# Batch 0 of an attention-and-FFN kernel: K and Q loaded by token halves, four-head chains, and new planner durations

## The chip, the cores and the metric

The kernel runs on one core of a Trainium2 chip. Its engines are TensorE (PE, matmuls; its weight loads are listed as PEld), VectorE (DVE), ScalarE (ACT), GpSimd (POOL) and SyncE (SP), which issues nearly all DMAs. The metric is the device time of one execution in microseconds, the median of three. Every engine works through its own list of instructions in order; semaphores join them.

## The reference

Sliding-window attention (window 32 to both sides) over 8 batches of 8 heads, 576 tokens and 64 features, followed by a feed-forward layer on 4608 tokens.

```python
scores = scale * np.matmul(q, k.transpose(0, 1, 3, 2))
mask = np.abs(pos[:, None] - pos[None, :]) <= window
scores = np.where(mask, scores, -1000000000.0)
scores = scores - np.max(scores, axis=-1, keepdims=True)
attn = np.exp(scores)
attn = attn / (np.sum(attn, axis=-1, keepdims=True) + 1e-09)
x = np.matmul(attn, v)            # then [tokens 4608, 512]
h = x @ w_in                      # 512 -> 2048
r = np.maximum(h, 0.0)
g = s * (r * r) + b
out = g @ w_out                   # 2048 -> 512
```

## The kernel before

The 4608 tokens are cut into 36 attention blocks of 128. A block needs its own 128 queries and the keys from 32 before to 32 behind it. The FFN takes 6 tiles of 128 tokens and 15 of 256. Its first layer (`s1`, line 1015) writes PSUM banks HT, two of them; ACT takes the relu (line 1024) into one of four R1 buffers; DVE squares it (line 1043) into GT; the second layer (`s2`, line 1063) sums 16 products of GT and WOUT in a bank, in four parts (one for each 512 rows of w_out, chunks o0 to o3); DVE scales and adds the bias vector CVEC (line 1077). A first-layer piece is 16 matmuls of 128 columns and needs one chunk of w_in (i0 to i3) and XT, the attention's output of its block.

**Order of the work.** The program builds a graph of nodes (`_Plan.add`), each with an engine or a choice of engines, a planned duration, a latency to its users and a key (its due time in tokens). `order` is a list scheduler: at each step the engine that is free first takes the ready node with the smallest key; with a choice of engines, a node is left to another engine if that one would end it sooner. The durations and the constants START to LAND decide the order in which each engine meets its instructions; on the chip only that order and the semaphores remain. In the first stage (`FILL`), gaps that the planner expects on PE are half filled with matmuls of ones (line 462), until a node with a tag changes the stage.

**Attention, ordinary path** (`attend`): 24 matmuls of 64 rows give the scores of 8 heads (line 820); DVE applies the mask and takes the maximum, head by head (line 832); ACT takes the exponential with its sum, head by head (line 840); the reciprocal of the sums (lines 846, 849); two multiplications of P by it (line 854, on POOL, or DVE for j under NDIV); P is transposed, on PE (line 877) for j under PDMA, else by a DMA (line 868); AV (line 892 for j under 12, later lines 909 and 915), and a copy into XT (line 900 or 926).

**Attention, transposed path** (`attend_light`, blocks j under LIGHT = 3): the scores with the mask summed in by a matmul (lines 691, 696), two maxima over four heads each (line 704), split into a high and a low bf16 part (708, 710), a second product that gives the scores transposed (716, 721), a transpose of the maxima (729), their subtraction by a selector PICK (740), two exponentials over four heads each (746), row sums (766, 768) and AV (757), the normalised result XN (775), transposed back (782) and copied into XT. All eight heads go through each step together.

**The first batch.** For its 576 tokens K and Q come by four loads (`load_raw`, K0 K1 Q0 Q1; line 571): a partition holds 36 neighbouring tokens of one head, and half 0 and half 1 are the first and last 18 of each. They are cast into FLAT (views of XT), turned by matmuls with a permutation (line 593) through five PSUM banks, and copied to TURN (lines 551, 556: the common lines of all casts and copies on DVE or POOL, and on ACT). Blocks 0 to 3 (WHOLE) read TURN and need all of it. Later K and Q come by `load_k` and `load_q`, are cast on POOL and turned on PE up to block KQDMA = 11, then by DMA.

**Loads** stand in one list, FIRST, and go out on SP in that order; the parts between the bars follow one attention block each. w_in and w_out are staged in slots that are parts of GT and OUTA, so a chunk waits until its slot was cast, and chunk i2 until Q's raw data was. WSET, VSET and OSET are the engines for the casts of the weights, of v, and of the second, shifted copy of v (VO). The scalars s and b are split in three bf16 parts (lines 473, 476) and spread by a matmul (482) with key SKEY; CVEC is made from column sums of WOUT (line 940) with key CKEY.

## Time and profile before

| what | us |
|---|---|
| median of three executions (316.78 to 318.54) | 316.85 |
| the profiled execution | 316.46 |
| its span in the trace | 314.7 |
| PE, DVE, ACT, POOL busy in the span | 300.8, 229.0, 230.0, 145.5 |
| first first-layer matmul starts | 21.32 |
| last exponential of block 3, copy of its XT | 38.15, 44.10 |

The span is a single execution, 1.76 us shorter than the time measured for it. In profile lines, `out<-in` names the tensors, x a count; the bracket at the end of a timeline line is the engine's idle time before it and who ended that. Matmuls are pipelined, so the durations of neighbours overlap, and distances from start to start are used for what one costs.

### The profile page before, as it was taken

The page shows a single profiled execution, that of the slowest core. Times are in us where ns is not written, and L with a number is a line of the kernel's source. Part 1 is how long each engine was busy: PE and PEld are TensorE (multiplying, and loading weights), DVE is VectorE, ACT ScalarE, POOL GpSimd, SP SyncE. Part 2 cuts the span into 40 slices and gives each one's busy share as a digit, 9 for nine tenths or more (in the row PEclk, how much of TensorE's full clock was granted, in tenths as well). Part 3 has the DMA queues.
Part 4 walks back from the last instruction along what each step waited for, and adds up shares of the span by engine and source line. Part 5 has one row for each costly group of instructions (what it writes and reads, how often), then busy time and mean ns, then how long its engine had stood idle before and what let it go on. Part 6 is the DMA issues. An engine that isn't in the chain of part 4 may idle for free.

```text
span 314.7 us, 10141 instructions
## 1 busy us (share of the span) xinstructions
PE 300.8 (96%) x3936; PEld 207.4 (66%) x3981; DVE 229.0 (73%) x897; ACT 230.0 (73%) x747; POOL 145.5 (46%) x192
## 2 busy tenths in 40 slices
PE   7899899998999999999999999999999999999996
PEld 3468657586667665776666766666666666676674
DVE  5779499899998778677766787678858767653242
ACT  5577866899797868698787878798878778835230
POOL 7233476556575534445454654655654532220000
PEclk9999999999999999999999999999999999999999
DMA  7998999999999999999999999899999562220011
GB/s 273 359 351 228 361 268 214 240 229 179 210 213 210 232 187 197 223 227 176 191 218 226 210 205 233 217 192 226 225 247 204 123 149 70 70 67 35 33 69 68
DMA packets 157125, 61.82 MB, mean 196 GB/s; under 512 B 131220, under 2 KB 147988, under 8 KB 157076
## 3 DMA queue, kind: packets, MB, share of 16 engines
q1 hardware_dynamic: 157072, 61.16, 90.7%
q8 instruction: 31, 0.51, 0.7%
q14 instruction: 18, 0.15, 0.2%
q10 hardware_dynamic: 4, 0.00, 0.0%
HBM read 37.03 MB, written 9.44 MB: 148 GB/s over the span
## 4 chain that ended last, share of the span: by engine, by line
PE 77%; DMA 7%; DVE 7%; ACT 3%; POOL 2%; issue 2%; SPq 1%
PE ht L1015 35%; PE ptp L1063 15%; PE outp L1063 15%; DMA gt<-in_moe_w_out_dram 3%; PE sc L820 3%; DMA v<-in_v_dram 2%; ACT p L840 2%; PE sc L1063 2%; DMA r32k<-in_k_dram 2%; PE av L1063 2%; DVE ss L832 1%; PE tp L909 1%; PE av L915 1%; DVE mx L704 1%; DVE outs L1077 1%
## 5 line engine op out<-in xcount | busy, mean ns | idle before, releaser
L1015 PE MATMUL ht<-xt,win 128*128 128x256 bf16 (+1 forms) x1344 | 146.5, 257 | 0.0
L1015 PEld LDWEIGHTS ht<-xt,win 128*128 128x128 bf16 x1344 | 115.1, 98 | 32.7
L1024 ACT ACTIVATE r<-ht 128x512 bf16<-128x512 f32 x144 | 85.1, 592 | 47.3 <-PE ht L1015 45.8
L1043 DVE TENSOR_TENSOR gt<-r 128x512 bf16<-128x512 bf16 x144 | 83.6, 583 | 48.7 <-ACT r L1024 47.1
L840 ACT ACTIVATE p<-ss,mx 128x128 bf16<-128x128 f32 x264 | 110.0, 420 | 7.6 <-DVE mx L832 6.9
L854 POOL TENSOR_TENSOR p<-p,rc 128x512 bf16<-128x512 bf16 x64 | 70.0, 1114 | 77.5 <-DVE rc L849 77.5
L832 DVE CUSTOM_DVE_ANT_0 ss<-sc,mask 128x128 f32<-128x128 f32 x264 | 62.0, 280 | 8.8 <-PE sc L820 8.4
L1063 PE MATMUL outp<-wout,gt 128*128 128x512 bf16 (+1 forms) x246 | 63.0, 372 | 3.9 <-issue 1.7
L1063 PE MATMUL ptp<-wout,gt 128*128 128x512 bf16 x240 | 61.9, 379 | 1.7 <-issue 1.3
L840 ACT ACTIVATION_READ_ACCUMULATOR p<-ss,mx 128x1 f32 x264 | 50.2, 190 | 0.0
L1063 PEld LDWEIGHTS outp<-wout,gt 128*128 128x128 bf16 x272 | 24.9, 98 | 19.3 <-ACT wout L556 1.0
L1063 PEld LDWEIGHTS ptp<-wout,gt 128*128 128x128 bf16 x256 | 24.1, 98 | 19.3
L551 POOL CAST kn<-r32k 128x512 bf16<-128x512 f32 x34 | 21.1, 646 | 23.9 <-DMA r32k<-in_k_dram 23.9
L551 POOL CAST qn<-r32q 128x512 bf16<-128x512 f32 x32 | 21.3, 665 | 9.9 <-DMA r32q<-in_q_dram 9.5
L832 DVE DVE_READ_ACCUMULATOR2_ANT mx<- 128x1 f32 x264 | 20.8, 79 | 0.0
L924 ACT COPY half<-tp 128x512 f32<-128x512 f32 x24 | 14.0, 583 | 9.2 <-PE av L915 8.8
L551 POOL CAST ve<-v 128x512 bf16<-128x512 f32 x27 | 18.0, 667 | 3.3 <-PE av L915 2.5
L926 DVE TENSOR_TENSOR xt<-av,half 128x512 bf16<-128x512 f32 x24 | 16.3, 681 | 0.9 <-ACT half L924 0.8
L820 PEld LDWEIGHTS sc<-kt,qt 64*64 64x64 bf16 x768 | 10.8, 108 | 8.7 <-issue 7.8
L820 PE MATMUL sc<-kt,qt 64*64 64x64 bf16 (+1 forms) x768 | 14.2, 204 | 0.0
L846 DVE TENSOR_SCALAR sm<-sm 128x8 f32<-128x8 f32 x33 | 6.7, 202 | 8.9 <-ACT p L840 8.8
L1077 DVE SCALAR_TENSOR_TENSOR outs<-outp,scb,cvec 128x512 f32<-128x512 f32 (+1 forms) x17 | 12.4, 728 | 0.9 <-PE outp L1063 0.9
(142 smaller groups left out, 237.3 us busy)
## 6 DMA issues: line engine op xcount, KB each, us to landing
out_dram<-outs SPq DMA_DIRECT2D x35, 256.0 KB, 3.8
v<-in_v_dram SPq DMA_DIRECT2D x28, 256.0 KB, 5.5
r32q<-in_q_dram SPq DMA_DIRECT2D x28, 256.0 KB, 5.2
r32k<-in_k_dram SPq DMA_DIRECT2D x9, 512.0 KB, 4.7
gt<-in_moe_w_in_dram SPq DMA_DIRECT2D x4, 1024.0 KB, 10.6
gt<-in_moe_w_out_dram SPq DMA_DIRECT2D x3, 1024.0 KB, 9.7
v<-in_v_dram SPq DMA_DIRECT2D x8, 192.0 KB, 5.1
r32k<-in_k_dram SPq DMA_DIRECT2D x3, 448.0 KB, 4.8
```

What stands on the lines that cost most here:

```text
L551: return e.tensor_copy(dst, src)
L820: r = e.matmul(SC[hh][64 * u:64 * u + 64, pr, x0:x1], lhsT=qq, rhs=kk, start=True, stop=True)
L832: lambda e, ss=ss, x=x, y=y, pr=pr, hh=hh: e.tensor_tensor_reduce(out=SS[ss][:, x, :], in0=SC[hh][:, pr, :], in1=MASK[kind][:, :], scale=- ...
L840: lambda e, ss=ss, x=x, y=y: e.activation(P[pb][:, y, :].rearrange("q (a p t) -> q a p t", a=2, t=2), spread(SS[ss][:, x, :]), AF.Exp, bia ...
L854: return e.tensor_tensor(P[pb][:, y0:y0 + 4, :], P[pb][:, y0:y0 + 4, :], RC[mb][:, y0:y0 + 4].unsqueeze(2).broadcast_to([128, 4, 128]), AL ...
L924: add("act", lambda e: e.copy(HALF[hb][:, :], AV2[:, :]), 620, key + AVK, reads=[AV2N], writes=[("HALF", hb)])
L926: add("dve", lambda e: e.tensor_tensor(XT[:, :, 128 * (j % NX):128 * (j % NX) + 128], AV[:, :, :], HALF[hb][:, :].rearrange("p (a b) -> p ...
L1015: r = e.matmul(hbank[:, nt * f:nt * f + nt], lhsT=WIN[:, kc, 128 * ft:128 * ft + 128], rhs=XT[:, kc, x0:x0 + nt], start=(kc == 0), stop=(k ...
L1024: return e.activation(R1[rb][:, :], hbank[:, :], AF.Relu, bias=0.0, scale=1.0)
L1043: return e.tensor_tensor(d, r, r, ALU.mult)
L1063: r = e.matmul(op_[:, 0:cn], lhsT=GT[:, g_, fc, :], rhs=WOUT[:, fc, c0:c0 + cn], start=(fc == 0), stop=(fc == 15))
L1077: add("dve", lambda e, ob=ob, op_=op_, c0=c0, cn=cn: e.scalar_tensor_tensor(OUTS[ob][:, 0:cn], op_[:, 0:cn], SCB[:, 0:1], CVEC[:, c0:c0 + cn],
```

## The change

K and Q of batch 0 are loaded by halves of the tokens: a load takes tokens 0 to 287 or 288 to 575 of all heads, 18 in a partition. Each half is cast and turned by itself, in three groups of six through three banks; blocks 0 and 1 depend on the first halves only. The second halves' casts have key HC, and their turns akey(2) - HT_ and a tag that ends the fillers. FLAT moves from XT to the buffers of SS and P. The list of loads becomes Q0 K0 K1 v0 v1 Q1 ..., o0 comes ahead of k2, q4, q5, and v4 behind o1.

The transposed path is used for two blocks, j = 0 and 1, and split in two chains of four heads (hh = 0, the even ones, and hh = 1), each with its own banks through to XN; the row sums and AV of a chain are one node with one bank (AV for hh = 0, TP for hh = 1). Only the back transpose takes both.

P of block 4 is turned on PE (PDMA 5). The scalars are split and spread behind block 1's XT. Casts of w_in and w_out may go to DVE too, casts of v only to POOL from block 4 on, half of VO to any of three engines; squares of the first 1536 tokens to DVE or POOL; the copies of turned K and Q up to j = 11 to ACT or DVE; normalisations of block 5 to DVE or POOL. The planner's latencies become 230 ns (ACT, DVE) and 190 (POOL) in place of 130; nearly all its durations are set anew (some shown), LAND, HOLD, L0, LS, RELU, SQ and the keys too. The look-ahead added to `order` has a window LOOK of 0.

```diff
-START, RING, ISSUE, LAND = 800.0, 2400.0, 700.0, 2000.0
+START, RING, ISSUE, LAND = 800.0, 2400.0, 700.0, 1200.0
...
-HOLD, DEFER, CHANGE = 800.0, 200.0, 97.0
+HOLD, DEFER, CHANGE = 1600.0, 200.0, 97.0
+LOOK, LOOK_GAP, LOOK_END = 0.0, 50.0, 60000.0
...
-        n = _Node(len(self.nodes), eng, fn, cost, 300.0 if eng == "pe" else 130.0, key, dsem,
+        n = _Node(len(self.nodes), eng, fn, cost, {"pe": 300.0, "pool": 190.0}.get(eng, 230.0), key, dsem,
...
-    LEAD, L0, LS = 640, 600, 60
-    RELU, SQ = 500, 200
-    FIRST = "K0 K1 Q0 Q1 v0 v1 i0 i1 i2 v2 i3 v3 v4|q4 o0 k2 o1 o2 q5 o3|v5|||"
+    LEAD, L0, LS = 640, 500, 40
+    NSQ = 12
+    RELU, SQ = 300, 400
+    FIRST = "Q0 K0 K1 v0 v1 Q1 i0 i1 i2 v2 i3 v3 o0|k2 q4 q5 o1 v4 o2 o3 v5||||"
     ANY = ("act", "dve", "pool")
...
-    WSET = {"i": ("pool", "act"), "o": ("act", "pool")}
-    NFLEX, TAIL = 8, 3
-    PDMA, KQDMA, AHEAD, GATE = 4, 11, 4, 5
-    CKEY, SKEY = 200, -9250
+    WSET = {"i": ("pool", "act", "dve"), "o": ("act", "pool", "dve")}
+    VOP = 12
+    HSTEP, CB, VOK = 0.1, -500, -100
+    NFLEX, TAIL = 12, 4
+    PDMA, KQDMA, AHEAD, GATE = 5, 11, 4, 5
+    CKEY, SKEY = 100, -300
     SLOT = dict(i0=0, i1=1, i2=2, i3=3, o0=2, o1=3, o2=4, o3=2)
     RAWNS = 1450
-    WHOLE, LIGHT, CH, NDIV = 4, 3, S // 16, 5
+    HC, HT_ = -8000, 400
+    WHOLE, LIGHT, CH, NDIV = 4, 2, S // 16, 6
...
     def VSET(j):
-        return ("pool", "dve")
-
-    def OSET(j):
-        return ("act", "dve")
+        return ("pool",) if j >= 4 else ANY
+
+    def OSET(j, r0):
+        return ANY if r0 == 0 and j < VOP else ("act", "dve")
...
-        FLAT = {x: XT[:, :, :].rearrange("p a b -> p (a b)")[:, o:o + CH * D]
-                for x, o in (("K", 0), ("Q", CH * D))}
+        FLAT = {"K": SSA[:, :, :, :].rearrange("p a b c -> p (a b c)").bitcast(BF16)[:, 0:CH * D],
+                "Q": PA[:, :, :, :].rearrange("p a b c -> p (a b c)")[:, 0:CH * D]}
...
-        PICK = sb((128, 8, 128), BF16, "pick")
+        PICK = sb((128, 4, 128), BF16, "pick")
...
-        for i in range(3):
-            add("dve", lambda e, i=i: e.tensor_copy(SC3[:, i, :], SC1[:, i, :]), 100, SKEY,
...
+            src = {"K": k, "Q": q}[x][0][:, S // 2 * half:S // 2 * half + S // 2, :].rearrange(
+                "h (c r) d -> h c (r d)", c=16)
...
+            turn_raw(x, half)
+
+        def turn_raw(x, half):
+            flat, out, late = FLAT[x], TURN[x], 0 if x == "K" else 50
+            step, n = CH * D // 8, CH // 6
+            ckey_, tkey = (-9500, -9400) if half == 0 else (HC, akey(2) - HT_)
+            for y in range(4 * half, 4 * half + 4):
+                lo = y * step
+                move(("act", "dve", "pool"), {"act": 360.0, "dve": 220.0, "pool": 440.0},
+                     flat[:, lo:lo + step], RAW[x][:, lo:lo + step], ckey_ + y + late,
+                     [("RAW", x, half)] + stage(x, half), [("FLAT", x, y)])
+            banks = ([(TPF, "TP"), (HT[0], ("HT", 0)), (PTPF, "PTP")] if x == "K" else
+                     [(AVF, "AV"), (OUTP, ("OUTP", 0)), (HT[0], ("HT", 0))]) if half == 0 else [
+                         (HT[(i + (x == "Q")) % 2], ("HT", (i + (x == "Q")) % 2)) for i in range(3)]
...
+                m = add("pe", fn, 58 * n, tkey + i + late,
+                        reads=["PERM"] + [("FLAT", x, y) for y in range(8)
+                                          if y * step < at + 64 * n and (y + 1) * step > at],
+                        writes=[res])
+                if half:
+                    m.tag = "turn"
...
-        turns = [("TURN", x, i) for x in "KQ" for i in range(5)] + ["KPAD"]
+
+        def turns(j):
+            return ["KPAD"] + [("TURN", x, half, i) for x in "KQ" for half in range(2 if j > 1 else 1)
+                               for i in range(3)]
...
+            AVB, avres = (AVF, TPF), ("AV", "TP")
+
+            def av(e, hh):
+                e.matmul(AVB[hh][:, 256:260], lhsT=EPS[:, :], rhs=ONES[:, 0:4], start=True, stop=False)
+                for y in range(hh, 8, 2):
+                    e.matmul(AVB[hh][:, 256 + y // 2:257 + y // 2], lhsT=PTS[ptb][:, y, :],
+                             rhs=ONES[:, 0:1], start=False, stop=False)
+                for u, vt in ((0, VE[ve]), (1, VO[vo])):
+                    for y in range(hh, 8, 2):
+                        c = 64 * (y // 2)
+                        r = e.matmul(AVB[hh][64 * u:64 * u + 64, c:c + 64],
+                                     lhsT=PTS[ptb][:, y, 64 * u:64 * u + 64],
+                                     rhs=vt[:, 64 * y:64 * y + 64], start=False, stop=(y == 6 + hh))
+                return r
...
             for hh in range(2):
+                h_ = hh * HSTEP
+                add("pe", partial(scores, hh=hh), 440, key + h_,
+                    reads=["B" + kind, "IDENT"] + turns(j), writes=[("SC", hh)])
...
+                    writes=[("MX", mb, y) for y in range(hh, 8, 2)])
+                mx = [("MX", mb, y) for y in range(hh, 8, 2)]
+                add("dve", lambda e, hh=hh: e.tensor_copy(M16[xb][:, hh, :, 0], MX[mb][:, hh:8:2]),
+                    150, key + 1 + h_, reads=mx, writes=[("M16", xb, hh, 0)])
+                add("dve", lambda e, hh=hh: e.tensor_tensor(
+                    M16[xb][:, hh, :, 1], MX[mb][:, hh:8:2], M16[xb][:, hh, :, 0], ALU.subtract),
+                    150, key + 1 + h_, reads=mx + [("M16", xb, hh, 0)], writes=[("M16", xb, hh, 1)])
+                st[hh] = add("pe", partial(scores_t, hh=hh), 500, key + 1 + h_,
+                             reads=["T" + kind, "IDENT"] + turns(j), writes=[sres[hh]])
             for hh in range(2):
+                h_ = hh * HSTEP
+                add("pe", partial(flip, hh=hh), 80, key + 1 + h_,
+                    reads=[("M16", xb, hh, 0), ("M16", xb, hh, 1), "IDENT"], writes=[("SC", hh)])
+                move(("act", "dve"), {"act": 150.0, "dve": 130.0}, MT[xb][:, hh, :],
+                     SC[hh][0:8, 0, 0:64].bitcast(BF16), key + 1 + h_, [("SC", hh)], [("MT", xb, hh)])
+                add("pe", partial(less, hh=hh), 240, key + 2 + h_, reads=[("MT", xb, hh), "PICK"],
+                    writes=[sres[hh]]).hard = st[hh]
...
+                turned[j] = add("pe", partial(av, hh=hh), 500, key + 3 + h_,
+                                reads=pts + [("VE", ve), ("VO", vo, 0), ("VO", vo, 64), "EPS", "ONES"],
+                                writes=[avres[hh]])
...
+        def spread_scalars(x1):
+            for i in range(3):
+                add("dve", lambda e, i=i: e.tensor_copy(SC3[:, i, :], SC1[:, i, :]), 100, SKEY,
+                    reads=["SC1"], writes=[("SC3", i)], after=[x1])
+                if i < 2:
...
+                if j == 1:
+                    spread_scalars(lastx[0])
...
-            stage = ([("W32", (g - 4) // 2, x) for g in range(max(4, g0), g0 + nt // 128)
+            stage = [("RAW", "K", x) for x in range(2)] if t0 < 384 else []
+            stage += ([("W32", (g - 4) // 2, x) for g in range(max(4, g0), g0 + nt // 128)
...
-                add("dve", sq, 440, key - SQ, reads=[("R1", rb)],
+                few = t0 < 128 * NSQ
+                add(("dve", "pool") if few else "dve", {"dve": sq, "pool": sq} if few else sq,
+                    {"dve": 400.0, "pool": 1100.0} if few else 400, key - SQ, reads=[("R1", rb)],
```

In the parts that are not shown the steps of `attend_light` (scores, scores_t, flip, less, the exponentials, reciprocal and XN) get an argument hh and work on the heads hh, hh + 2, hh + 4, hh + 6; the remaining lines set durations, among them relu 600 to 490, square 440 to 400, exponential 390 to 413, casts 620 / 425 / 640 to 525 / 385 / 560 (ACT / DVE / POOL).

254 lines of the change are left out of this document (110 added, 144 removed).

## The prediction

> **What bounds the kernel now.** I read the page's busy shares, then busy time by stretch, the same table for the filler matmuls of line 462 alone, TensorE's timeline around the first FFN matmuls, its waits, and one VectorE group in two stretches. The page's first row puts TensorE (PE) at 96% of the span, so I ask where the other 4% and the work that isn't the FFN lie.
>
> Busy time by stretch; columns: PE, weight loads, DVE, ACT, POOL, granted clock, DMA share, GB/s.
>
> ```profile
> 6.60:11.60 5.00, 4.07 (x147) 2.99 (x146) 4.21 (x12) 4.42 (x10) 2.66 (x5) 1.00 1.12 339
> 11.60:21.30 9.70, 8.55 (x181) 4.61 (x181) 6.05 (x16) 4.83 (x10) 3.40 (x6) 1.00 1.07 389
> 21.30:45.00 23.70, 21.76 (x398) 17.81 (x393) 19.10 (x52) 18.31 (x45) 11.51 (x17) 1.00 1.01 296
> 45.00:80.00 35.00, 33.33 (x514) 23.13 (x508) 32.80 (x143) 29.26 (x109) 22.04 (x28) 1.00 1.14 216
> 100.00:264.00 164.00, 161.47 (x2057) 110.78 (x2082) 122.05 (x531) 131.82 (x459) 84.36 (x105) 1.00 1.06 201
> ```
>
> The same, for the fillers of line 462 alone (PE first):
>
> ```profile
> 6.60:11.60 5.00, 0.92 (x3) 0.19 (x2) 1.00 1.12 339
> 11.60:21.30 9.70, 1.38 (x4) 0.30 (x4) 1.00 1.07 389
> ```
>
> From 100 us on PE lacks 2.5 us in 164, and the clock is 1.00: that stage is bound by matmuls which the change doesn't touch. Before the first FFN matmul (21.32 us) PE is idle or runs fillers for (5.00 - 4.07 + 0.92) + (9.70 - 8.55 + 1.38) = 4.4 us of 14.7. From 21.3 to 80 us it is idle 1.94 + 1.67 = 3.6 us. So the end is the sum of PE's work plus these gaps, and the change can act only before 80 us.
>
> The timeline of PE (start, duration):
>
> ```profile
> 11.65 0.60 PE L691 MATMUL sc<-maskb,ident 128*128 128x512 bf16 x2 [0.44 <-DVE qwt L551]
> ...
> 20.41 0.61 PE L691 MATMUL sc<-maskb,ident 128*128 128x512 bf16 x2
> 20.94 0.45 PE L696 MATMUL sc<-kwt,qwt 64*64 64x128 bf16 x24
> 21.32 1.96 PE L1015 MATMUL ht<-xt,win 128*128 128x128 bf16 x32
> ...
> 27.77 0.45 PE L820 MATMUL sc<-kwt,qwt 64*64 64x128 bf16 x24
> 28.14 1.96 PE L1015 MATMUL ht<-xt,win 128*128 128x128 bf16 x32
> ```
>
> Block 0 waits until 11.65 us for all four halves of K and Q to be cast and turned; blocks 0, 1, 2 take the transposed path, block 3 (L820) the ordinary one.
>
> **Part 1, block 2 leaves the transposed path.** From start to start on PE, a transposed block costs: scores 20.41 to 21.32, 0.91; transposed scores 23.94 to 24.85, 0.91; flip of the maxima (L729) 0.15; their subtraction (L740) 27.22 to 27.77, 0.55; sums and AV (L766 to L757) 23.12 to 23.94, 0.82; back transpose (L782) 25.75 to 26.07, 0.32; together 3.66. Ordinary block 3: scores 0.37, turn of P (L877) 40.78 to 41.23, 0.45, AV (L892) 0.44; together 1.26. PE saves **2.4 us**. It adds, off PE, eight exponentials on ACT (0.40 from start to start, 3.2 us, against two of 0.59), eight masks on DVE (0.21 each), two normalisations and one more copy. ACT has 5.4 us free in 21.3 to 45 and DVE 4.6, so these are hidden there; without that cover the extra 2 us of ACT would show.
>
> **Part 2, the two chains.** The 24 small matmuls of L696 take 0.38 us, 16 ns each, because they alternate between the upper and lower 64 rows. A chain of four heads uses one half of the rows. Nearest row: L892 (43.39 and 43.54), which alternates only between column halves and starts eight 64-column matmuls in 0.15 us, 19 ns each. Twelve matmuls of a chain are 16 such units: 0.30 us, so 0.61 for both chains against 0.38, +0.24. Scores and transposed scores of two blocks are four such pairs: **+1.0 us**. From below 0; from above, with no overlap (28 ns for 64 columns, 55 for 128, half the 0.056 us per 128-column matmul of L1015 for the smaller), 0.44 per chain, +2.0. I take 1.0, the row with the same column halves. The merged sums and the smaller subtraction keep their matmul counts: nothing.
>
> **Part 3, P of block 4 turned on PE** in place of a DMA transpose: one more L877 group, **+0.45**, and a 0.68 us copy; SP loses one transpose with its wait.
>
> **Part 4, scalars moved off the start.** DVE spends 4.57 to 6.15 us splitting s and b (L473, L476), first waiting 1.1 us for their DMA, while the first half has landed by 5.14 (POOL casts it then); PE's first turn is at 6.67. Without these, DVE casts from 5.2 on and the turn can start by 6.2: **-0.5** (0 to -0.7). Behind block 1 they lie beside DVE's gaps before 21 us, and CVEC, their only user, is made at 50 us.
>
> **Part 5, halves by tokens.** Blocks 0 and 1 need only Q0 and K0, the first two transfers (landed at 5.1 and about 6.1 us by POOL's casts of 5.14 and 6.24). Casts 0.8, turns 0.8 and evictions 0.6 to 0.7 put scores at about 8.4 in place of 11.65. The second halves' casts and turns (now with keys ahead of block 0's attention) share ACT and DVE with the chain. Block 0 took 11.65 to 20.38 for its XT, of which 0.6 was ACT behind the w_in cast (15.17) and 1.3 DVE behind block 1's maximum. With the early start and two chains overlapping, XT of block 0 comes at about 15 to 16, before the first w_in chunk is cast (16.3). The transfers ahead of w_in are the same bytes, so w_in chunks still land at 15.2, 17.7, 20.2 and 24.3, and FFN matmuls fill in behind them from 16.4. I let the 4.4 us of gaps and fillers shrink to 2.0: **-2.4**. The second halves' turns carry the tag that ends the fillers, so those 1.38 us after 11.6 go; no row shows a clock under 1.00 to price a colder PE by, and with gaps as short as these I put it at nothing. Bounds: 0 (gaps merely move), -3.4 (only the latency before the first scores, 1 us, is left).
>
> **Part 6, order of loads, sets of engines, planner's durations.** Two PE waits:
>
> ```profile
> PE outp L1063 <- POOL wout L551: 0.9, 1, 0.9
> PE tp L667 <- POOL qn L551: 0.5, 1, 0.5
> ```
>
> The first is w_out's second chunk: it waits for its transfer, then for two casts in a row on each of ACT and POOL (36.72 to 37.89). Fewer bytes now stand ahead of the first chunk (v4 and q4 go behind it), the same ahead of the second (q5 for v4), but DVE may take a share of the casts, 0.43 each, which ends them some 0.4 us sooner. Another qn wait of 1.0 us lies at 77.5: with the 0.5 and the 0.9, 2.4 of the 3.6 us are waits for a cast on POOL. Casts of v leave DVE for POOL, some squares too, and the planner will think DVE freer than it is (a square planned at 400 ns is measured at 583 over the run). I take a fifth of the 2.4 as gone, **-0.5**, between -2.0 and +2.0, about half the gaps seen. HOLD should change nothing: scores and AV stand together already in the steady stage, and the 0.16 us issue gaps there stay. TAIL only changes which nodes are listed first; the banks of the last tiles are the same.
>
> Sum: -2.4 + 1.0 + 0.45 - 0.5 - 2.4 - 0.5 = **-4.35 us**. The profiled execution took 316.46 (span 314.7, 1.76 around it); it would take 312.1, span 310.35. The median 316.85 lies 0.39 above the profiled execution: **312.5 us**.
>
> A rule that speaks against the change stands in the Trainium skill, "SBUF — State Buffer", section "Who interferes with whom": a VectorE instruction with two SBUF inputs and a GpSimd instruction reading SBUF exclude each other, and the later one blocks for the whole of the other. The trace agrees in kind. First row: 45 to 80 us, POOL busy 63%; second: 285 to 300 us, POOL idle.
>
> ```profile
> L1043 DVE TENSOR_TENSOR gt<-r 128x512 bf16<-128x512 bf16 x13 | 7.8, 615 | 0.1
> ...
> L1043 DVE TENSOR_TENSOR gt<-r 128x512 bf16<-128x512 bf16 x7 | 3.0, 425 | 8.4 <-ACT r L1024 8.4
> ```
>
> **Rivals.**
>
> *The gap moves.* The work gained before 26 us only ends earlier at the wait for w_out: no FFN block can finish before its last chunk (issued at 32.96, cast from 43.38), and ordinary blocks 2 and 3 are slow (block 3: scores 27.77, XT copied 44.10). For it: ACT and DVE are 77 to 81% busy in 21.3 to 45 and 84 to 94% in 45 to 80. Against: by 44 us there are 16 first-layer pieces of 0.87 us for blocks 0 to 3 and six second-layer ones, more than PE did. Parts 4 and 5 (2.9) and part 6 (0.5) are then given back: 312.5 + 3.4 = 315.9. Chance 0.20.
>
> *POOL blocks DVE.* Eligible squares: 24 of the first six tiles and 24 of the next three. If half go to POOL at the 1.1 us of its normalisation (L854, 1095 ns), each holding a DVE operation up for 0.3 us on average (half of 0.6), DVE loses 24 x 0.3 = 7 us against 24 x 0.615 = 15 relieved, so the sum is fine; what costs is order. POOL waits 6.2 us for q and k loads in 45 to 80 (kn 2.5, qn 3.7), and a square queued behind such a wait holds a bank of HT, of which there are two. Eight such stalls of 1.0 us, the qn wait of 77.5, give 312.5 + 8 = 320.5, slower than before. It decides once PE's gaps in 21.3 to 80 exceed 3.6 + 4.35, about 8 us. Against it: POOL is 63% busy, four R1 buffers stand between. Chance 0.09.
>
> *More than I count.* Gaps down to the bound of part 5 (-1.0) and part 6's -2.0 (-1.5), with part 2 at 0 (-1.0): 309.0. Chance 0.13.
>
> **How the numbers follow.** Forecast 0.58, with its own range 310.5 to 314.8. The range 308.7 to 316.8 takes in the first and third rivals and leaves out the second and the outer ends. A difference under 1% (313.7 to 320.0) can hardly be told from none. Faster: 0.50 of the forecast's 0.58, and the third rival's 0.13: 0.63. Slower: 0.06 of the second rival's 0.09, as 320.5 sits on the bound. Same: 0.31.
>
> **What would show it.** Scores of block 0 near 8.4 us and the first L1015 near 16.4, if part 5 is right; two chains' 12 small matmuls near 0.30 us each; block 2 in L820; fewer L462 fillers; no wout wait of 0.9; squares on POOL near 1.1 us, and PE's gaps in 21.3 to 80 at most 3.6 us; the stretch from 100 us on unchanged but for its start. It is wrong if the first L1015 comes early and PE's gaps in 21.3 to 45 grow by as much, or if waits for POOL squares appear on ht or outp.

## The result and the profile after

| | us | executions |
|---|---|---|
| after, median | 336.66 (335.42 to 337.55) | 6 |
| before, median, same chip | 316.62 (315.80 to 318.54) | 6 |
| ratio | 1.061, 95% interval 1.058 to 1.064 | |
| span of the profiled execution, after | 334.1 (before 314.7) | 1 |

The changed kernel is 6.1% slower, where 312.5 us was forecast. In the runs below, executions over 1.5% longer than the fastest of the same kernel are left out of the ratios, though not of the medians: two of ten of before_row_halves, one of ten of before_cold, three of four of after_whole_loads, which so has no ratio, and, on three of the chips, one to four executions of the kernel before.

Busy time by stretch, changed kernel, in the columns of the prediction's first table (PE, weight loads, DVE, ACT, POOL, granted clock, DMA share, GB/s):

```profile
6.60:11.60 5.00, 2.14 (x38) 1.17 (x38) 0.75 (x2) 1.85 (x5) 0.56 (x1) 1.00 0.70 148
11.60:21.30 9.70, 5.49 (x107) 3.79 (x109) 4.50 (x13) 3.58 (x7) 1.74 (x3) 1.00 0.76 193
21.30:45.00 23.70, 20.80 (x328) 15.38 (x325) 13.68 (x59) 13.54 (x40) 5.89 (x9) 1.00 0.87 263
...
100.00:264.00 164.00, 160.05 (x1994) 110.33 (x2019) 125.03 (x530) 130.95 (x458) 90.54 (x111) 1.00 1.16 211
```

From 100 us on little differs; the loss lies at the start. Between 6.6 and 21.3 us TensorE has 7.6 us of work where it had 12.6, and all other engines are emptier too. The last column points to the cause, which the runs below test: 148 and 193 GB/s against 339 and 389.

The timeline of the engines that cast, in the changed kernel (start, duration; the bracket is the idle time before and what ended it):

```profile
8.64 0.75 DVE L554 CAST p<-gt 128x288 bf16<-128x288 f32 x2 [5.18 <-DMA gt<-in_q_dram]
12.94 0.97 DVE L554 CAST ss<-gt 128x288 bf16<-128x288 f32 x3 [3.54 <-DMA gt<-in_k_dram]
16.17 0.97 DVE L554 CAST ss<-gt 128x288 bf16<-128x288 f32 x3 [2.26 <-DMA gt<-in_k_dram]
23.11 0.75 DVE L554 CAST p<-gt 128x288 bf16<-128x288 f32 x3 [2.04 <-DMA gt<-in_q_dram]
25.36 1.17 POOL L554 CAST win<-gt 128x512 bf16<-128x512 f32 x2 [7.15 <-DMA gt<-in_moe_w_in_dram]
```

Read from the top: Q0 at 8.64 us, K0 at 12.94, K1 at 16.17, Q1 at 23.11, and the first chunk of w_in at 25.36, against 15.17 before. Every one of these casts waited for a DMA.

TensorE's timeline in the changed kernel, same columns:

```profile
9.29 0.53 PE L600 MATMUL av<-perm,p 128*64 128x64 bf16 x12 [4.04 <-POOL p L554]
...
13.59 0.53 PE L600 MATMUL tp<-perm,ss 128*64 128x64 bf16 x12 [2.17 <-POOL ss L554]
...
16.98 0.85 PE L600 MATMUL ht<-perm,ss 128*64 128x64 bf16 x24 [2.22 <-DVE ss L554]
17.77 0.61 PE L701 MATMUL sc<-maskb,ident 128*128 128x512 bf16 x1
...
23.59 0.85 PE L600 MATMUL ht<-perm,p 128*64 128x64 bf16 x24 [0.68 <-ACT p L559]
...
33.56 1.89 PE L1048 MATMUL ht<-xt,win 128*128 128x128 bf16 x16 [0.52 <-DVE xt L554]
```

TensorE stands 9.1 us in four waits for casts of K and Q. The third is a wait of order: the turn of K1, which block 0 doesn't need, stands ahead of block 0's scores (17.77) and waits for casts that begin at 16.17. The first FFN matmul comes at 33.56 us, 12.2 later than before, and sixteen of them take 1.89 us, or 1.82 from their start to the start of the next matmul; before, they took 1.07, or 0.90 (24.85 to 25.75). A mask matmul of 512 columns takes 0.61 us, against 0.38 to 0.39 before. The kernel before had such slow matmuls too, but only in its first 6 us:

```profile
5.04 0.63 PE L462 MATMUL ht<-ones 128*128 128x512 bf16 x1
...
6.35 0.39 PE L462 MATMUL ht<-ones 128*128 128x512 bf16 x1
...
24.85 1.07 PE L1015 MATMUL ht<-xt,win 128*128 128x128 bf16 x16
```

Its first clock record begins at 6.1 us. In the changed kernel TensorE runs at half clock until 38 us, although the clock column reads 1.00 there: this trace has no clock record before 38 us. (The trace of after_joint, below, has records in that part: 0.50 in 11.6 to 21.3 us, and there a 512-column matmul takes 0.61 us as well.) So a clock of 1.00 in a table of stretches means full speed only where the trace holds a record, and the length of a known matmul tells.

### The profile page after: what moved, and what is told of

It reads as the page before. It is cut to its first block, busy times and chain, and to the rows that moved or that the text cites. A ratio compares the mean times of both kernels' runs of the same rounds, so it can differ in the third digit from the quotient of the medians.

```text
span 334.1 us, 10121 instructions
## 1 busy us (share of the span) xinstructions
PE 308.7 (92%) x3898; PEld 212.9 (64%) x3945; DVE 232.6 (70%) x922; ACT 230.2 (69%) x760; POOL 150.9 (45%) x195
## 4 chain that ended last, share of the span: by engine, by line
PE 70%; DVE 15%; ACT 5%; DMA 5%; issue 2%; SPq 2%; DVEq 0%
PE ht L1048 31%; PE outp L1098 14%; PE ptp L1098 13%; DMA gt<-in_q_dram 5%; DVE gt L1076 4%; ACT p L852 4%; PE sc L832 3%; DVE ss L844 3%; PE sc L1098 2%; PE av L1098 2%; DVE p L866 1%; ACT r L1057 1%; DVE vo L554 1%; SPq L534 1%; DVE wout L554 1%
## 5 line engine op out<-in xcount | busy, mean ns | idle before, releaser
L1048 PE MATMUL ht<-xt,win 128*128 128x256 bf16 (+1 forms) x1344 | 149.8, 260 | 2.4 <-DVE xt L912 0.9
L1048 PEld LDWEIGHTS ht<-xt,win 128*128 128x128 bf16 x1344 | 116.4, 99 | 37.9 <-ACT r L1057 1.9
L852 ACT ACTIVATE p<-ss,mx 128x128 bf16<-128x128 f32 x272 | 113.3, 419 | 12.8 <-DVE mx L844 12.1
L866 POOL TENSOR_TENSOR p<-p,rc 128x512 bf16<-128x512 bf16 x64 | 72.5, 1151 | 102.5 <-DVE rc L861 94.0
L844 DVE CUSTOM_DVE_ANT_0 ss<-sc,mask 128x128 f32<-128x128 f32 x272 | 64.2, 281 | 11.2 <-PE sc L832 10.4
L852 ACT ACTIVATION_READ_ACCUMULATOR p<-ss,mx 128x1 f32 x272 | 51.6, 190 | 0.0
L554 POOL CAST ve<-v 128x512 bf16<-128x512 f32 x34 | 24.5, 721 | 8.8 <-PE av L927 6.3
L554 POOL CAST kn<-r32k 128x512 bf16<-128x512 f32 x34 | 21.8, 668 | 7.9 <-DMA r32k<-in_k_dram 6.1
L1112 DVE SCALAR_TENSOR_TENSOR outs<-ptp,scb,cvec 128x512 f32<-128x512 f32 x16 | 11.9, 741 | 3.0 <-PE ptp L1098 2.8
```

Source lines behind the costliest of these rows:

```text
L554: return e.tensor_copy(dst, src)
L844: lambda e, ss=ss, x=x, y=y, pr=pr, hh=hh: e.tensor_tensor_reduce(out=SS[ss][:, x, :], in0=SC[hh][:, pr, :], in1=MASK[kind][:, :], scale=- ...
L852: lambda e, ss=ss, x=x, y=y: e.activation(P[pb][:, y, :].rearrange("q (a p t) -> q a p t", a=2, t=2), spread(SS[ss][:, x, :]), AF.Exp, bia ...
L866: return e.tensor_tensor(P[pb][:, y0:y0 + 4, :], P[pb][:, y0:y0 + 4, :], RC[mb][:, y0:y0 + 4].unsqueeze(2).broadcast_to([128, 4, 128]), AL ...
L1048: r = e.matmul(hbank[:, nt * f:nt * f + nt], lhsT=WIN[:, kc, 128 * ft:128 * ft + 128], rhs=XT[:, kc, x0:x0 + nt], start=(kc == 0), stop=(k ...
L1112: add("dve", lambda e, ob=ob, op_=op_, c0=c0, cn=cn: e.scalar_tensor_tensor(OUTS[ob][:, 0:cn], op_[:, 0:cn], SCB[:, 0:1], CVEC[:, c0:c0 + cn],
```

## The experiments

Ratios are to the kernel before on the same chip, with their 95% interval. Names with before_ are edits of the kernel before, names with after_ edits of the changed one; whole_joint is an edit of the changed kernel too, and two_light_again repeats before_two_light.

### How a load is spread and walked

**after_sixteen.** The changed kernel's source has the eight heads as its outermost dimension, the kernel before had (head, chunk) merged to 128. Here the chunk goes outermost, with the permutation to match.

```diff
-                "h (c r) d -> h c (r d)", c=16)
+                "h (c r) d -> c h (r d)", c=16)
...
-                [[-16 * sg, 2], [-32 * sg, NPAIR], [-sg, 16]], 0, sg, 0.0,
+                [[-sg, 2], [-2 * sg, NPAIR], [-8 * sg, 16]], 0, sg, 0.0,
```

> The changed kernel with the four K and Q loads reading their source as 16 chunks by 8 heads in place of 8 heads by 16 chunks (the permutation matrix follows; every byte, order and duration of the planner stays). Theory A, that a load whose outermost source dimension is 8 uses half of the 16 DMA engines: the first casts of Q come at about 5.2 us in place of 8.64, w_in's first chunk is cast near 16 in place of 25.4, PE stays at 380 ns for a 512-column matmul, and the time is 310 to 315 us. Theory B, that the missing fillers make PE slow whatever the loads do: loads early as in A, but 608 ns matmuls until 25 us or later, 318 to 326 us. Theory C, that the two chains and the new order lose it: loads early, PE fast, and still 325 us or more.

Measured: 329.82 us, ratio 1.034 (1.029 to 1.039). The same stretch, 4 to 6 us, in the kernel before, in the changed kernel and in this one:

```profile
4.00:6.00 2.00, 1.67 (x6) 0.32 (x4) 1.30 (x5) 0.86 (x3) 1.56 (x3) 1.00 1.02 410
```

```profile
4.00:6.00 2.00, 1.25 (x5) 0.27 (x3) 0.00 (x0) 0.27 (x1) 0.28 (x1) 1.00 0.59 164
```

```profile
4.00:6.00 2.00, 1.25 (x5) 0.27 (x3) 0.15 (x1) 0.42 (x2) 0.40 (x2) 1.00 1.06 251
```

The share of the 16 DMA engines in use goes from 0.59 to 1.06: with eight heads outermost the loads got by with about half of the engines. That is 2.7 of the 6.1%. But 251 GB/s isn't the 410 of before in that stretch: the packets of 4608 bytes took 304 ns at the median, against 178 before, and the first chunk of w_in is cast at 19.04 us. None of the three theories holds whole: the loads come sooner, though not as soon as theory A has them, TensorE is slow as in B, and the time is that of C.

**before_eight.** The reverse: the kernel before, each load cut in two with eight heads outermost (and the permutation to match).

```diff
-            src = {"K": k, "Q": q}[x][0].rearrange("h (c r) d -> (h c) (r d)", r=CH)
+            src = {"K": k, "Q": q}[x][0].rearrange("h (e c r) d -> e h c (r d)", e=2, r=CH)
...
-            lastload[0] = add("sp", lambda e: [e.dma_start(RAW[x][:, lo:hi], src[:, lo:hi])], 500,
+            lastload[0] = add("sp", lambda e: [e.dma_start(RAW[x][64 * u:64 * u + 64, lo:hi], src[u, :, :, lo:hi]) for u in range(2)], 500,
```

> The kernel before, with each of its four K and Q loads issued as two DMAs of 64 partitions whose source is 8 heads by 8 chunks; all other instructions and their order are those of before. Theory A: half of the DMA engines carry these loads, K's second half lands 3 to 4 us later, w_in's first chunk about 8 to 10 us later, and the time rises to 325 to 336. Theories B and C: the loads are not at fault, 316 to 319.

Measured: 327.07 us, ratio 1.023 (1.017 to 1.029). Loads with eight heads outermost, with nothing else of the change, cost over 7 us:

```profile
4.00:6.00 2.00, 1.81 (x6) 0.27 (x4) 1.11 (x5) 0.53 (x2) 1.38 (x3) 1.00 0.51 134
...
11.60:21.30 9.70, 2.90 (x73) 2.20 (x73) 2.44 (x6) 3.06 (x6) 1.58 (x3) 1.00 0.68 154
```

A DMA share of 0.51, 134 GB/s, and TensorE idle for 6.8 of 9.7 us. These packets took 273 ns at the median, so the 2.3% holds slow packets as well as idle engines. The first chunk of w_in is cast at 25.61 us and the first FFN matmul starts at 34.60, both later than in the changed kernel (25.36 and 33.56), and yet this kernel loses 2.3%, not 6.1: late loads alone are not the whole loss.

**before_chunk_first.** Whole-token loads of before on all 16 engines, but in the row order of after_sixteen (the permutation follows again).

```diff
-            src = {"K": k, "Q": q}[x][0].rearrange("h (c r) d -> (h c) (r d)", r=CH)
+            src = {"K": k, "Q": q}[x][0].rearrange("h (c r) d -> c h (r d)", r=CH)
```

> The kernel before with its four K and Q loads walking 16 chunks by 8 heads in place of 8 heads by 16 chunks; the same bytes, halves, engines and order. If the order in which 16 DMA engines walk the source sets the packet's time (304 ns for 4608 bytes in the run with 16 chunks, 178 before): packets near 300 ns, the four loads end about 3.5 us later, 319 to 324. If it is the token halves (pieces 4608 bytes apart) that slow them: 178 ns and 316 to 319.

Measured: 321.96 us, ratio 1.012 (1.004 to 1.020), packets 308 ns, DMA share 1.02 and 240 GB/s in 4 to 6 us.

**before_same_walk.** The rows of before in their old order, written with three dimensions, 16 x 8 x 1152.

```diff
-            src = {"K": k, "Q": q}[x][0].rearrange("h (c r) d -> (h c) (r d)", r=CH)
+            src = {"K": k, "Q": q}[x][0].rearrange("h (e c r) d -> (h e) c (r d)", e=2, r=CH)
```

> The kernel before with the same four loads, the same rows in the same order to the same partitions, but the source written with three dimensions, 16 x 8 x 1152, in place of 128 x 1152. It tells two readings of the slow packets of after_sixteen and before_chunk_first (median 304 and 308 ns against 178) apart. Theory 'the walk': 16 engines, each with 8 neighbouring rows of one head as before, packets at 178 ns, the four loads landed within 6.7 us of the first packet as before, time within 1 us of before. Rival 'the three-dimensional form': packets near 300 ns, the loads 3 us longer, time 320 to 322.

Measured: 318.77 us, ratio 1.002 (0.997 to 1.006); packets 178 ns at the median, 387 GB/s. So the slow packets don't come from the number of dimensions but from the order in which the rows of the source are walked. Which property of the order does it stays open: before_eight takes neighbouring rows of a head one after the other, as before, and its packets were slow all the same. No trace shows which DMA engine took which rows.

### Fillers and a cold start

**after_fillers** lets the fillers run on past the second halves' turns; **after_sixteen_fillers** does so on top of after_sixteen.

```diff
-                if half:
-                    m.tag = "turn"
```

> The changed kernel without the tag that ends the fillers at the turn of the second halves; loads as they are. Theory A: the loads stay late (first cast 8.64, w_in 25.4), a filler or two more cannot bridge gaps of 4 us, so 512-column matmuls stay at 608 ns until about 30 us and the time is 333 to 337. Theory B: fillers bring PE to 380 ns from 17 us on and the time falls to 326 to 330. Theory C: no difference, 336.

> Both edits: loads over 16 chunks, and no tag that ends the fillers. Theory A: within 1 us of the run with 16 chunks alone, 310 to 315. Theory B: 5 us or more below that run. Theory C: 325 or more.

Measured: 336.62 us, ratio 1.055 (1.050 to 1.060), and 329.54, ratio 1.033 (1.028 to 1.038): each as its kernel without the edit. The tag isn't the cause. It is a weak test of the fillers, though, as the planner adds a single one (11 in place of 10). The second run shows something else: its clock is back at full at 32.2 us, where that of after_sixteen is back at 39.5, and the profiled executions take 329.66 and 329.76 us. A clock 7.3 us sooner changed nothing that can be measured.

**after_sixteen_warm** adds 17 filler matmuls to after_sixteen: five ahead of the turn of Q0, seven at that of K0, five between those of K0 and K1.

```diff
+    WARM = {"Q0": 5, "K0": 7, "K1": 5}
...
+                    add("pe", warm, 100, -9410 + 200 * half + late, reads=["ONES"], writes=[wres], after=turnedraw[-1:] if half else [])
```

> The kernel with loads over 16 chunks, and 17 more filler matmuls of 512 columns that write banks not yet in use: 5 ahead of Q0's turn, 7 in it, 5 between the turns of K0 and K1. Theory A: granted clock 1.00 from 6 us on, so the light blocks and first FFN pieces take half the time, and the run of 329.8 falls to 317 to 322; what is left above 313 is late loads. Theory B', that a busy PE regains its clock by itself and the half clock from 9 to 40 us costs nothing that is not hidden: 328 to 330.

Measured: 328.56 us, ratio 1.033 (1.022 to 1.043), where after_sixteen has 1.034: nothing that can be told apart, as theory B' had it. The clock record shows full speed from about 6.5 to 20 us and then half until 30. The clock bought with fillers ahead of the scores is lost again before the FFN starts; the first FFN matmul comes at 26.23 us in place of 27.41.

**before_cold** takes the fillers of the kernel before away (one in place of seven, and none in the gaps).

```diff
-FILL, FILL_MIN, FILL_SHARE, FILL_NS = ("attn", "sums"), 400.0, 0.5, 220.0
+FILL, FILL_MIN, FILL_SHARE, FILL_NS = ("attn", "sums"), 400.0, 0.0, 220.0
...
-        add("pe", lambda e: fill(e, "attn", 7), 2990, K0, reads=["ONES", "NIL"]).tag = "attn"
+        add("pe", lambda e: fill(e, "attn", 1), 2990, K0, reads=["ONES", "NIL"]).tag = "attn"
```

> The kernel before with one filler in place of the seven at the start and none in the gaps; order and all other work the same. If the fillers are what brings PE to full clock: 512-column matmuls at 608 ns and granted clock 0.5 until 25 to 40 us, 323 to 330. If the clock comes up by itself with the first dense work: 315 to 318.

Measured: 318.45 us, ratio 0.998 (0.994 to 1.002), with a mean granted clock of 0.74 in 11.6 to 21.3 us and 0.89 in 21.3 to 45. A clock that is half for part of the first 27 us cost nothing that shows in this kernel, and so the 15 fillers that were taken away bring nothing either.

### The row halves

**before_row_halves.** The kernel before with the 12 matmuls of one row half first and the 12 of the other behind, in place of alternating.

```diff
-                for pr in range(NPAIR):
-                    for u, x0, x1, y0 in ((0, 0, 128, 0), (1, 64, 128, 64), (1, 0, 64, 128)):
-                        for hh in range(2):
-                            r = e.matmul(SC[hh][64 * u:64 * u + 64, pr, x0:x1],
+                    for pr in range(NPAIR):
+                        for u, x0, x1, y0 in ((0, 0, 128, 0), (1, 64, 128, 64), (1, 0, 64, 128)):
+                            r = e.matmul(SC[hh][64 * u:64 * u + 64, pr, x0:x1],
```

> The kernel before with only the order of the small score matmuls changed: in the three transposed blocks the 12 of the upper row half first, then the 12 of the lower, in place of alternating. This is part 2 of the prediction alone. By the prediction's step: 0.24 us for each of six pairs, +1.4 us, the clock unchanged: 318.0 against 316.6. Theory 'a chain of one row half is what lets the clock fall': the granted clock drops to 0.5 somewhere in 12 to 28 us and the time rises by 3 to 6 us, to 320 to 323. Rival 'in-order overlap hides it': within 0.5 us of before.

Measured: 318.77 us, ratio 1.001 (0.996 to 1.005), where the forecast 1.4 us can't be told from none; the eight executions behind it all had a mean clock of 1.00. The other two took 326.7 and 326.8 us at a mean clock of 0.97. The profile is one of these; its clock record reads half from about 12 to 32 us.

```profile
11.60:21.30 9.70, 9.68 (x108) 4.95 (x103) 3.92 (x10) 4.04 (x8) 3.52 (x7) 0.51 1.07 385
```

TensorE is busy all the time, the transfers are at full rate, and the clock (0.51) still doesn't come back. Two of ten against none so long in 30 executions of the kernel before on that chip (321.2 us at most) is a hint and settles nothing.

**after_sixteen_joint.** after_sixteen with the scores of a block in one node and row halves alternating again, for the scores and the transposed scores; all else stays in two chains.

```diff
-                add("pe", partial(scores, hh=hh), 440, key + h_,
-                    reads=["B" + kind, "IDENT"] + turns(j), writes=[("SC", hh)])
+                if hh == 0:
+                    add("pe", scores, 880, key, reads=["B" + kind, "IDENT"] + turns(j),
+                        writes=[("SC", 0), ("SC", 1)])
...
```

> The changed kernel with the chunk dimension outermost in the loads (as in after_sixteen) and with the score matmuls of a transposed block in one node, alternating between the upper and lower 64 rows. Theory 'chains of one row half hold the clock down': the granted clock, 0.5 from 8.9 to 39.6 us in after_sixteen, is back at 1.00 by 20 to 25 us, first FFN matmul by 25 us, time 322 to 326 (the 3.9 us of before_chunk_first and some 2 us of the rest stay). Rival 'the late, slow loads alone': clock at 0.5 until past 30 us as before, time 328 to 330.5.

Measured: 323.48 us, ratio 1.015 (1.008 to 1.023), 6.3 us under after_sixteen. First after_sixteen, then this kernel, by stretch:

```profile
11.60:21.30 9.70, 9.70 (x148) 6.18 (x148) 4.76 (x16) 5.48 (x12) 1.77 (x3) 0.50 1.04 346
21.30:45.00 23.70, 21.72 (x307) 17.55 (x307) 17.31 (x71) 13.40 (x39) 8.97 (x12) 0.62 0.87 237
```

```profile
11.60:21.30 9.70, 9.21 (x177) 5.72 (x178) 6.15 (x19) 4.98 (x10) 2.48 (x3) 0.50 1.06 335
21.30:45.00 23.70, 19.33 (x317) 15.29 (x319) 19.45 (x77) 17.72 (x53) 11.43 (x16) 0.86 1.03 291
```

Up to 21.3 us both run at half clock. There a chain with its mask takes 1.10 us (17.77 to 18.87 in the changed kernel), so 2.2 a pair, and the alternating pair 1.54 (12.58 to 14.12). Four pairs are 2.6 us, and by as much the first FFN matmul comes sooner, at 24.79 us in place of 27.41. The clock record is back at full near 28 in place of 39.5. The theory's time came (322 to 326), its mechanism in part: the clock wasn't back by 25, and what its return is worth isn't shown, as after_sixteen_fillers gained nothing from one 7.3 us sooner. The edit also makes one node of two, and the list scheduler's order moves with that, so the rest of the 6.3 us stays open.

**after_joint.** The same edit in the changed kernel as it is, loads on eight engines.

> The changed kernel with only the score matmuls of a transposed block put back into one node, alternating between the upper and lower 64 rows; the loads stay as changed, on eight engines. Theory 'chains of one row half cost 6 us through the clock, wherever the scores lie': about 330 against 336.7, the clock at 1.00 by 30 us in place of 38.5. Rival 'with eight engines the loads end so late that nothing else counts': 335 to 337.

Measured: 336.95 us, ratio 1.055 (1.050 to 1.060), against 1.061 (1.058 to 1.064) for the changed kernel: nothing that can be told apart. The rival holds. First FFN matmul 33.22 us, 0.3 sooner. While the loads set the pace, the shorter scores gain nothing; the same edit is worth 6 us once the loads come sooner. The costs don't add up part by part.

### What is left with the loads of before

**after_whole_loads.** The changed kernel with the four whole-token loads and turns of before, in their order; the rest of the change stays.

```diff
-    FIRST = "Q0 K0 K1 v0 v1 Q1 i0 i1 i2 v2 i3 v3 o0|k2 q4 q5 o1 v4 o2 o3 v5||||"
+    FIRST = "K0 K1 Q0 Q1 v0 v1 i0 i1 i2 v2 i3 v3 o0|k2 q4 q5 o1 v4 o2 o3 v5||||"
...
-                "h (c r) d -> h c (r d)", c=16)
+            src = {"K": k, "Q": q}[x][0].rearrange("h (c r) d -> (h c) (r d)", r=CH)
```

> The changed kernel with part 5 undone alone: K and Q of batch 0 loaded, cast and turned as before (whole heads, 36 tokens in a partition, list K0 K1 Q0 Q1 v0 v1), everything else of the change kept (two chains, two blocks, scalars moved, planner's durations, sets of engines). Theory A, the new loads and the PE clock that goes cold behind them are the whole loss: K0 cast near 5.2 us, granted clock 1.00, time 313 to 317. Theory C, the chains or the planner's new order lose time too: loads early, clock 1.00, and 320 us or more. If the clock drops here too, without late loads, it is the fillers.

Measured: 317.50, 323.51, 323.74 and 324.72 us; the mean clock was 0.999 in the first and 0.979 to 0.989 in the others. The first is just above theory A's range, the others are in C's, though with the clock below 1.00. The profile (324.72) shows what the chains cost at full and at half clock:

```profile
11.48 0.39 PE L693 MATMUL sc<-maskb,ident 128*128 128x512 bf16 x1 [0.42 <-DVE qwt L554]
11.80 0.44 PE L697 MATMUL sc<-kwt,qwt 64*64 64x128 bf16 x12
12.17 0.39 PE L693 MATMUL sc<-maskb,ident 128*128 128x512 bf16 x1
12.49 0.44 PE L697 MATMUL sc<-kwt,qwt 64*64 64x128 bf16 x12
12.86 0.39 PE L704 MATMUL ptp<-maskt,ident 128*128 128x512 bf16 x1
...
18.82 0.61 PE L704 MATMUL ptp<-maskt,ident 128*128 128x512 bf16 x1
19.36 0.63 PE L708 MATMUL ptp<-qwt,kwt 64*64 64x64 bf16 x12
19.92 0.61 PE L704 MATMUL outp<-maskt,ident 128*128 128x512 bf16 x1
```

From start to start, 12 small matmuls of one row half take 0.37 us (11.80 to 12.17), and the pair with its masks 1.38 (11.48 to 12.86), against 0.91 alternating: +0.47 a pair at full clock. Behind the second block's scores the clock fell, near 18 us, and a chain took 1.10 (18.82 to 19.92).

**whole_joint.** after_whole_loads with the row halves alternating (the edit of after_sixteen_joint).

> The changed kernel with the whole-token loads of before (as in after_whole_loads) and, besides, the scores of a transposed block as one node again: the 24 small matmuls alternate between the upper and the lower 64 rows, for the scores and for the transposed scores; maxima, flips, subtractions, exponentials and AV stay in two chains. Theory 'a chain of one row half is what lets the clock fall': with row halves alternating the granted clock stays at 1.00 between 17.9 and 24.7 us, the 24 matmuls take 0.38 to 0.45 us in place of 2 x 0.56, and the time is 315 to 317.5, at least 3 us under the usual 323.6 of after_whole_loads. Rival 'the clock falls for want of FFN work there': the clock falls again near 18 us in most executions and the time is 321 to 324. Rival 'the rest of the change loses it elsewhere (casts, planner)': clock at 1.00 and still 318 or more.

Measured: 320.68 us, ratio 1.007 (1.003 to 1.012), clock 0.989 to 1.000. In the profile the clock falls for one stretch of 3.4 us. The last rival holds: with full-rate loads and no row halves, what is left of the change still costs 0.7%.

**before_two_light**, and **two_light_again** with more rounds: the kernel before with two blocks on the transposed path, part 1 alone.

```diff
-    WHOLE, LIGHT, CH, NDIV = 4, 3, S // 16, 5
+    WHOLE, LIGHT, CH, NDIV = 4, 2, S // 16, 5
```

> The kernel before with the transposed path for two blocks in place of three and nothing else: part 1 of the prediction alone. By the prediction's step: PE saves 2.4 us and ACT hides 3.2 us of exponentials, so 314.2 to 315. Rival 'ACT or DVE shows': block 2's path from scores to XT is longer by its 16 head-by-head steps on DVE and ACT, PE waits for its XT, and the time is 316.5 to 319.

> before_two_light once more, against the kernel before, as the one version that measured under both (ratio 0.997, interval 0.9933 to 1.0006). Theory 'part 1 is worth about 1 us': ratio 0.995 to 0.999 with an interval that ends below 1. Rival 'nothing': an interval on both sides of 1.

Measured: 317.15 us, ratio 0.997 (0.993 to 1.001), and 317.81, ratio 0.997 (0.994 to 0.9997): some 0.3%, about 1 us, at the edge of what these runs can tell from none. The forecast step (314.2 to 315) didn't come; the first rival's time did. The stretch where the 2.4 us were to be saved, and ACT's timeline in it (before_two_light):

```profile
21.30:45.00 23.70, 19.49 (x320) 15.06 (x321) 18.94 (x67) 18.80 (x55) 10.28 (x15) 1.00 1.02 297
```

```profile
27.43 0.59 ACT L1024 ACTIVATE r<-ht 128x512 bf16<-128x512 f32 x1
27.91 0.42 ACT L840 ACTIVATE p<-ss,mx 128x128 bf16<-128x128 f32 x1
...
29.56 0.42 ACT L840 ACTIVATE p<-ss,mx 128x128 bf16<-128x128 f32 x1
...
29.98 0.58 ACT L1024 ACTIVATE r<-ht 128x512 bf16<-128x512 f32 x1
```

TensorE's busy time falls by 2.27 us (21.76 to 19.49); the stretch has a fixed length, so its idle time grows by as much. Five exponentials of block 2 in a row hold the relu back from 27.9 to 29.98 us; with two HT banks TensorE then waits 1.44 us for it (30.61). The trace of two_light_again has the same five exponentials and the same wait (29.71); the kernel before has none there.

**before_light_loads** adds part 6's loads to before_two_light, **before_light_scalars** part 4.

```diff
-    FIRST = "K0 K1 Q0 Q1 v0 v1 i0 i1 i2 v2 i3 v3 v4|q4 o0 k2 o1 o2 q5 o3|v5|||"
+    FIRST = "K0 K1 Q0 Q1 v0 v1 i0 i1 i2 v2 i3 v3 o0|k2 q4 q5 o1 v4 o2 o3 v5||||"
-    WSET = {"i": ("pool", "act"), "o": ("act", "pool")}
+    WSET = {"i": ("pool", "act", "dve"), "o": ("act", "pool", "dve")}
```

```diff
-    CKEY, SKEY = 200, -9250
+    CKEY, SKEY = 200, -300
...
+                if j == 1:
+                    spread_scalars(lastx[0])
```

> before_two_light (transposed path for two blocks) with, besides, the changed kernel's list of loads from i0 on (o0 ahead of k2, q4, q5; v4 behind o1) and DVE allowed for the casts of w_in and w_out: part 6's loads alone. By the prediction's step: the wait of TensorE for w_out, 1.3 us in before_two_light, shrinks by about 0.5 us: 316.6 against 317.15. Rival 'casts on DVE delay the attention': waits for XT or for DVE grow, 318 or more.

> before_two_light with the splitting and spreading of the scalars moved behind block 1's XT: part 4 alone. By the prediction's step: the first turn starts 0.5 to 1.1 us sooner and the time falls by 0.5 us, to 316.6. Rival 'Q's second half sets the start of the scores': the first turn starts near 5.6 us in place of 6.67, the scores of block 0 still at 11.6 (the last transfer lands at 8.7), and TensorE waits 0.6 to 1.2 us for the scalars later: 317.2 to 318.2.

Measured: 317.35 us, ratio 0.999 (0.996 to 1.002), and 317.77, ratio 0.999 (0.996 to 1.002). Neither adds to part 1. In the first, w_out's wait fell from 1.3 to 0.3 us, and these waits of TensorE are new:

```profile
PE tp L782 <- DVE xn L775: 1.2, 1, 1.2
PE av L892 <- DVE pts L551: 0.9, 1, 0.9
```

The first of them has the cause that its rival named: VectorE casts two pieces of w_in (20.55 to 21.62 us) just ahead of block 0's XN (L775).

In the second the first turn began at 6.46 us (6.67 in before_two_light), and block 0's scores at 12.71 us. The two traces without the move have them at 13.11 and 12.19, so they don't start sooner; and TensorE waits 0.7 us for the scalars later, where it waited 0.5 at the start. Its rival holds in the main, though the first turn did not come as early as it said.

These starts show how far executions differ. In six traces of the kernel before and of its edits with its loads (before, before_two_light, two_light_again, before_light_loads, before_row_halves, before_same_walk), POOL begins to cast the last of the four loads at 9.25 to 10.76 us, and block 0's scores follow 2.3 to 2.9 us behind it, at 11.65 to 13.11. The 11.65 of the profile before is the earliest of the six.

## Why the prediction was wrong

**The step that failed** is in part 5: "The transfers ahead of w_in are the same bytes, so w_in chunks still land at 15.2, 17.7, 20.2 and 24.3", and with it the landings of Q0 and K0 at 5.1 and 6.1 us. The bytes are the same, the shape isn't. The new source keeps 8 as its outermost dimension where the old one merged to 128, and the loads used about half of the DMA engines, at 148 to 164 GB/s in place of 339 to 410. They came at 8.64 and 12.94 us, w_in at 25.36. The diff shows this in one line. The Trainium skill, "DMA: Bandwidth & Descriptors", section "Why a DMA increments its semaphore by 16 and not by 1", says that the number of engines is the largest one up to 16 that divides the slowest dimensions of both access patterns. By that rule eight heads give eight engines, and the trace agrees (share 0.59 and 0.51 against 1.02 before). What it doesn't give is the other part of the loss, packets of 258 ns at the median here, and of 273 to 332 in the other kernels with a new row order, in place of 178; that shows in the runs alone.

**Scores of block 0 at 8.4 us.** They came at 17.77. Besides the loads, the step took dependencies for order: block 0 needs only Q0 and K0, but TensorE had K1's turn ahead of its scores and waited 2.22 us for it.

**"I put it at nothing"**, the colder clock. Its reason, "no row shows a clock under 1.00", doesn't hold: the fillers of the kernel before take 0.63 us up to 5.04 us and 0.39 from 6.35 on, so its own trace had the price. For the fillers, nothing was the right value (before_cold). For the rest the term was not small: at half clock a chain takes 1.10 us in place of 0.69, and sixteen FFN matmuls 1.89 in place of 1.07, until 38 us. How much of the 20 us that is stays open. after_sixteen_warm with full clock until 20 us and after_sixteen_fillers with the clock back 7.3 us sooner are no faster than after_sixteen.

**Part 2, +1.0 us.** On TensorE the mechanism holds, the size doesn't: 0.37 us for a chain's 12 matmuls against the 0.30 taken, and two masks apart take 0.64 in place of 0.53, so +0.47 for each of four pairs, +1.9 us, next to the upper end of 2.0. In the time it doesn't show at full clock: six pairs in before_row_halves would be 2.2 us by the small matmuls alone (an estimate, 0.36 each), and its interval ends at 1.6. With loads on 16 engines and the clock at half, the same edit undone is worth 6.3 us (after_sixteen_joint), of which 2.6 are the shorter scores; with eight engines nothing (after_joint).

**Part 1, -2.4 us.** TensorE has the less work, as said; about 1 us of it arrives. "ACT has 5.4 us free ... so these are hidden there" was a mean over 23.7 us; the relu behind five exponentials is late where it matters. This is the rival that the gap moves, for this part.

**Part 4, -0.5 us, and part 6, -0.5 us.** Both nothing in the runs. K's turn was not on the path: the last of the four loads (Q1, cast from 9.22 us in the kernel before) sets the start of the scores, which follow it by 2.3 to 2.9 us in six traces. Of w_out's wait 1.0 us went, and two of 1.2 and 0.9 us appeared, the first of them behind casts of w_in that DVE was now allowed.

**Part 3, +0.45 us,** wasn't tried alone, nor were the planner's latencies and HOLD; they and the sets of engines are in the 0.7% of whole_joint, and how that divides stays open. The trace of whole_joint doesn't tell: its scores of block 0 begin at 12.58 us, within the 11.65 to 13.11 of the six traces above.

**Squares on POOL,** the rival that ended slower, did not occur: all 144 squares of the changed kernel ran on DVE (583 ns each, as before). Slower was given 0.06, for a reason that did not occur; no rival had the loads themselves in it.

**Where the 6.1% went,** undone one after the other: sixteen engines 2.7 (1.061 to 1.034), scores in one node with row halves alternating 1.8 (to 1.015), whole-token loads in the row order and list order of before 0.8 (to 1.007), the rest 0.7. The shares hold for this order alone: with eight engines the second is nothing, and loads with eight heads outermost, put alone into the kernel before, cost 2.3, the row order 1.2. The ratios have intervals of 0.3 to 0.7% to either side and come from several chips, so the 0.8 is not clear of the noise.

## What to carry to other kernels

When a diff touches the source of a load, count its dimensions from the outside before its bytes: with 8 outermost the DMA share was 0.51 to 0.59, with 16 or 128 about 1, and the order of the rows decided whether a packet took 178 ns or 300. At the start of a kernel take a DMA share near 0.5 in the stretch table as the sign of it, and cost a new order of small matmuls at half clock too. An early operand is worth nothing on an in-order engine while a late one stands ahead of it. And before a shift of under 1.5 us at the start is read from one trace, see how far traces of kernels with the same start differ.

## What the hardware showed that was not expected

- Packets of the same 4608 bytes took 178 ns at the median in one row order (before_same_walk) and 308 in another (before_chunk_first), with the source in three dimensions and a DMA share of about 1 in both.
- TensorE busy all the time did not bring its clock back: 9.70 of 9.70 us at 0.50 in after_sixteen, at half from about 9 to 39.5 us. The Trainium skill, "TensorE: Matmul & The Clock Gate", section "What's actually happening", has the clock at full after some 3.4 us of sustained work. This trace doesn't agree for small and half-row matmuls. Behind the first FFN matmul it took 12 us there, 27.41 to 39.5, two of them into the first unbroken run of 48 FFN matmuls (from 37.08). In four other traces it took 3.2 to 4.6 us (33.56 to 37.9 in the changed kernel, 24.79 to 27.9 in after_sixteen_joint, 26.23 to 30.4 in after_sixteen_warm, 27.60 to 32.2 in after_sixteen_fillers), which is nearer to the page. As a busy TensorE in the profile isn't one at its peak, this does not show what the gate counts.
- When the clock falls differs between executions of one kernel: in two of ten of before_row_halves the mean clock was 0.97 and in the others 1.00, in three of four of after_whole_loads 0.979 to 0.989 and in one 0.999. No run shows why.
